# Mixing step of batches 1 to 3 with cosine and sine sums kept apart over half the columns

## The chip, the cores and the metric

The kernel runs on one NeuronCore of one Trainium2 chip. The metric is the device time of one execution in microseconds (us), measured beside the kernel before on the same chip. Before the change the median of three runs is 973.34 us (965.94 to 981.02).

## What is computed

The reference chains a recurrent attention layer, a Fourier mixing layer with a two-layer network, and a network that mixes tokens and then channels. The change touches the Fourier layer alone:

```python
X = np.fft.fft(x, axis=1)          # x: (4, 768, 320): batch, token, feature
X = np.fft.fft(X, axis=2)
mixed = np.real(X)
u = x + mixed
mu = mean(u, -1); var = mean((u - mu) ** 2, -1)
un = (u - mu) / np.sqrt(var + 1e-06)
out = u + np.maximum(un @ w_ch1, 0.0) @ w_ch2
```

The real part of the second transform is a cosine sum minus a sine sum. Over 320 output features the cosine sum is even (column j and column 320-j agree) and the sine sum is odd.

## The kernel before

The program is one list of some 4,500 operations. Each is declared with a cost and the data it reads and writes; the order in which all are issued, over all engines, is a table of base-36 numbers written out in the file (`ORDER`). An entry such as `+5,acc,0` is a filler: five products of an identity matrix (function `warm`, L54) into a PSUM bank that nobody reads. Each engine takes its instructions in that order, and waits on semaphores.

In time the program runs through these stages: the attention (to about 395 us); the first Fourier step and mixing of batch 0 (to 430.6); the channel network of the Fourier layer (430.6 to 682.5), in six groups of four 128-token tiles, each a chain of `hps` products (L1049, 8 of 512 columns), a relu on ScalarE (L1051), its low part on VectorE (L1052), and `acc` products (L1039, 12 of 320 columns); the token network (`tps`, `t2ps`, to 730); and the last channel network (`sa`, `sb`, `acc` L1075). Batches 1, 2 and 3 pass their Fourier step between the products of groups 0, 2 and 3. Each number is split into a high and a low part (fp32r), so that one exact product is three rounded ones.

Function `fft2` is the mixing step. Its loop makes four blocks `mix` for each batch. A block is eight matmuls of 322 columns into one PSUM bank of the pair `mm` (shared with `hps` and with the transposes `trp`): A0, A1 are the high and low parts of the cosine rows, A2, A3 those of the sine rows, A4 the 64 remaining rows, and T2 the table of cosines and sines in six slabs. VectorE then adds the block to the tile X, read straight from PSUM, and for all but part of the tiles a second time with the columns reversed (L952, seven adds for each batch; each also leaves the row sum). ScalarE squares and sums each tile (`sq`, L955). From the sums VectorE forms `v`, `y`, `q` and `nb` (L962 to L969), the shift and scale of the batch; `norm` and `trp` (L1020) use them to make the operand `cc` of the next group. Only batch 1 is followed at once by a group that needs it (group 1, at 481.5 us); batches 2 and 3 are needed one group later.

While this runs, the weights of the second network are decoded on VectorE and GpSimd (tiles `mdraw`, `mdt`, `mda`, `mdh`, L854 to L860). GpSimd also issues the loads of weights from DRAM (`wload`): T2 at 390 us, W1 (`W1t`) and W2 from 402 us.

Of the kernel before, what the change touches and what calls it, by code (L numbers as in the profile page):

```python
# [539 lines left out]
+10,y,0 7w:0 88:1 89 8b:1 8c 7z:1 8d dt 7x +1,y,0 85:0 ds bs bt 80 82:1 83 3b 86 8e 8f 7y 8g 8j 8i 8k hk 8h dy du dr dz 3c 3e 8w 84 81 3d 8x 8y +7,y,0  # L540
8z:1 90 95:0 96 98:1 99 9b:0 9c 92:1 93 9e:0 9f 9j 3f 3i 3j 9i 3g 3m 3h 3n 8a bw bv 87 3k dv dw c6 9a 3l 3o e0 hl hr dx e3 e1 e2 hm 9h hq hn ho mp hs
ms 3r 3p 9k 9o 9p 9q 9r 9s 9t 9u 9v 9w 9x 9y 42 43 9z a0 mt 91 +12,y,0 e4:1 e5 9n +2,y,0 e7:0 e8 c9 3q a1 a4 a2 a3 a5 a6 a8 a9 9l aa a7 +2,y,0 ed:1 bu
b5 b3 b8:2 b9 ba bb bc bd fi b6 e9 ab ad b7 ee ef ac 44 9m b4 ew +2,y,0 ej:0 ek el +3,y,0 be:0 +1,y,0 bf bg bh ea:1 eg:0 et ey:1 ez ae af bi bj +2,y,0
cb:2 +2,y,0 ce:0 ex ah qj eb 94 f0 +1,y,0 f1 e6 ag ai aj al hj hp eh en em ep 9d cc cd cf cg +2,y,0 ct:1 cm:2 cn co ch:0 ck cl ci cj cp cq f3 cr:0 f2
f4:1 f5 f6 +1,y,0 f7 cu ak am ap aq an at ao au eo es eq er hv cs cy:1 d6:0 cz cv:1 cw d0 d1 fy:0 hu ec fh eu ar as f8 d7 d8 ax ht ev g0 fv:2 of hw:0
i5:1 av 45 4a cx:0 ay aw b2 d9 fz 97 46 48 fx d2 i6 i7 i2:1 9g hx d3:0 f9 mq i3 i4 ib:1 az b0 b1 g4:0 d4 i8:0 gh:1 fw g1:1 ic id hz:1 47 49 4c 4d 4e
4g 4h 4b g6 i9 g5 ia hy gi g3 k0 gj i0 i1 if ie g2 d5 gc:2 gf gg df:0 ig dg dh di 4f 4i 4j gk dc:1 dd fj fk fl fm gl:0 gm g7:0 ga gb da nw ih k5:1
+2,m,0 k6 k7 k8 k9 ka ns +1,m,0 gn:1 go db +2,m,1 de:0 dj dk dl dn kh:0 ki g8 g9 k3 +1,m,0 fn:1 fo gd ge il im in io ip iq ir is it iu iv +2,y,0 kj:0
kk ei fp:1 fq h0:1 h1 h2 h3 dm l5:1 l2:0 k2 gx:0 gy l4 fr:0 gp:1 gq iw fs ft:1 fu mu dp l3 gs:0 l7 do gt gu gv k1 k4 l6 ix iy kp mv mw to kl:0 mr km
kb:2 kc kd ke gr:0 gw gz h4 kf kg lb:0 n0 iz ij n1 j1 h5 h6:1 n2 lc ko h9:0 nx:1 ld h7 kq j0 ha +1,t,0 h8:0 kr hb j2 hc l8:2 kt ii ik j5 hd l9 o9:1 oh  # L550
j3 la ny oa j6 nz o0 vq nu ob:0 j7 o1 mx o2 ls:1 ja oc n6:1 j4 od:0 he lt j8 oe hf n3:0 j9 ql jb ks qk ku:1 nv le:0 my kv je hg lo:0 hh mz lu:1 lj:2
4m lv qm n7 og kw:1 n4 lz:1 lq jc 4l n5 nt jd m0 +1,y,0 nc:0 lf kx m2 lm lw:1 4k nd m1 lg ky:1 lx nf:0 ln kz jf ng ji +1,y,0 l0:1 ni:1 lp lh n9:0 nh
o3:1 lr lk li o4 nj o5 na o6 nk qn l1 o7 nm ou:0 qo nl o8 m4:1 zi ow m7:0 m5 qp m8 +1,t,0 ly:0 qq jg md:1 qw ma jh no m3 m9 me qu ll m6 jj qv mg:0 4n
oi oj mb qs ox:2 qr mh jk nn mc mi qx:1 mj jl n8 ok oz np jo +1,y,0 r0:0 jp nr mf:0 js ov qy ol mk 4o nq jm pg:1 r1 jn ti:0 xg oy tq jq p0:1 pi tj jr
+1,m,0 r3:1 4p ju ph r6:0 qz ml r4 mm nb jt pj mo p3:0 r5 jv r7 mn p1 jz qt p2 4q vr r8 jw +5,y,0 om:0 vt +2,y,0 r9:1 tk:1 4s on rc:0 jy ra vu p6:2 jx
# [118 lines left out]
TC=416  # L674
# [6 lines left out]
def tables():  # L681
# [625 lines left out]
```

## Time and profile before

| | us |
|---|---|
| median of 3 runs | 973.34 |
| lowest, highest | 965.94, 981.02 |
| the profiled execution's own time | 981.04 |
| its span, first to last instruction | 979.3 |
| busy: TensorE (PE) | 926.0 (95%) |
| busy: VectorE (DVE) | 710.4 (73%) |
| busy: ScalarE (ACT) | 491.7 (50%) |
| busy: GpSimd (POOL) | 371.4 (38%) |

All durations below come from the profiled execution. An instruction's duration includes its passage through the engine's pipeline; how long a matmul holds up the next one is read from the difference between two starts. "x8" in a row of the timeline merges eight like instructions that follow each other.

### The profile page before, as it was taken

The numbers are of one execution on the slowest core, as the hardware profiler recorded it, in microseconds if no ns is written. First come the engines' busy times: TensorE is split into PE (matmuls) and PEld (weight loads), VectorE is DVE, ScalarE is ACT, GpSimd is POOL, SyncE is SP. The second block draws the span as 40 slices with busy tenths as digits, with TensorE's granted clock in tenths as the row PEclk, the third lists the DMA queues.
The fourth block names the chain that finished last, engine by engine and source line by source line (L and its number), as shares of the span: only waits on it lengthen the run. The fifth ranks groups of instructions, "written<-read, shape, count | busy, mean of one in ns | idle before, by whom it ended". The sixth has DMA issues, their size and how long they took to land.

```text
span 979.3 us, 24229 instructions
## 1 busy us (share of the span) xinstructions
PE 926.0 (95%) x9661; PEld 858.9 (88%) x9661; DVE 710.4 (73%) x1543; ACT 491.7 (50%) x1068; POOL 371.4 (38%) x498
## 2 busy tenths in 40 slices
PE   7568999999999999889999999999999999999998
PEld 6467888888898888779898998989999999999998
DVE  6798469798886936998978776562686876666554
ACT  5254688879788766352444443322324443433422
POOL 5121344535266355426265644254243213122110
PEclk9775699999999999999999999999999999999999
DMA  9877488989978799657344434349533212303000
GB/s 217 165 143 162 105 176 195 194 181 195 205 193 169 202 213 308 208 202 228 115 152 120 158 112 124 108 131 379 181 137 119 86 51 78 97 4 98 1 28 28
DMA packets 153840, 146.15 MB, mean 149 GB/s; under 512 B 101695, under 2 KB 127359, under 8 KB 152959
## 3 DMA queue, kind: packets, MB, share of 16 engines
q1 hardware_dynamic: 143743, 117.64, 47.1%
q0 software_dynamic: 9984, 26.96, 9.0%
q8 instruction: 76, 1.25, 0.6%
q14 instruction: 37, 0.30, 0.1%
HBM read 96.22 MB, written 43.58 MB: 143 GB/s over the span
## 4 chain that ended last, share of the span: by engine, by line
PE 71%; DVE 12%; DMA 7%; ACT 3%; issue 2%; SPq 1%; POOL 1%; DVEq 0%; ACTq 0%; POOLq 0%
PE acc L1075 12%; PE hps L1049 11%; PE acc L1039 10%; PE sb L1086 7%; PE sa L1086 5%; PE kg L216 4%; PE sc L406 3%; PE warm L54 3%; PE tps L1181 2%; PE t2ps L1194 2%; PE mix L949 2%; DVE pr L249 2%; DMA RT<-a 2%; DMA Mst<-Md 1%; SPq L134 1%
## 5 line engine op out<-in xcount | busy, mean ns | idle before, releaser
L1049 PE MATMUL hps<-cc,W1t 128*128 128x512 f32 x480 | 121.0, 395 | 0.1
L1039 PE MATMUL acc<-W,cc 128*128 128x320 f32 x720 | 116.0, 310 | 0.0
L1039 PEld LDWEIGHTS acc<-W,cc 128*128 128x128 f32 x720 | 109.2, 188 | 4.7 <-ACT mdh L838 0.3
L1049 PEld LDWEIGHTS hps<-cc,W1t 128*128 128x128 f32 x480 | 87.8, 188 | 16.9 <-PE hps L1049 0.5
L1099 POOL TENSOR_TENSOR C<-C,C 128x256 f32<-128x256 f32 x36 | 27.4, 761 | 173.0 <-DVE W1t L1092 115.3
L1051 ACT ACTIVATE cc<-hps 128x512 fp32r<-128x512 f32 x60 | 35.8, 597 | 107.0 <-PE hps L1049 107.0
L54 PE MATMUL warm<-ident 128*128 128x128 f32 x490 | 82.1, 307 | 2.6 <-POOL ident masks.py:199 2.0
L1052 DVE SCALAR_TENSOR_TENSOR cc<-hps,cc 128x512 fp32r<-128x512 f32 x60 | 41.3, 689 | 55.6 <-ACT cc L1051 55.5
L54 PEld LDWEIGHTS warm<-ident 128*128 128x128 f32 x490 | 71.2, 213 | 5.5 <-POOL ident masks.py:199 2.0
L225 POOL TENSOR_SCALAR_AFFINE_SELECT RT<-RT 64x384 f32<-64x384 f32 (+1 forms) x66 | 44.1, 687 | 80.8 <-ACT RT L136 79.7
L216 PE MATMUL kg<-am,bt 120*128 120x192 f32 x242 | 59.7, 388 | 15.1 <-ACT am L136 13.6
L416 POOL TENSOR_SCALAR_AFFINE_SELECT sc<-sc 64x384 f32<-64x384 f32 (+1 forms) x72 | 41.7, 579 | 79.1 <-ACT sc L136 75.6
L1093 DVE TENSOR_TENSOR C<-sb,C 128x256 f32<-128x256 f32 x108 | 44.2, 420 | 33.2 <-PE sb L1086 26.4
L1075 PE MATMUL acc<-v,W1t 128*128 128x320 f32 x432 | 67.4, 309 | 0.1
L1075 PE MATMUL acc<-vb,W1t 128*128 128x320 f32 x432 | 66.9, 309 | 0.0
L1091 ACT ACTIVATE W1t<-C 128x256 fp32r<-128x256 f32 x108 | 41.9, 413 | 45.4 <-DVE C L1093 36.4
L1075 PEld LDWEIGHTS acc<-v,W1t 128*128 128x128 f32 x432 | 63.7, 188 | 0.4 <-DVE W1t L1092 0.4
L1075 PEld LDWEIGHTS acc<-vb,W1t 128*128 128x128 f32 x432 | 63.7, 188 | 0.0
L216 PEld LDWEIGHTS kg<-am,bt 120*128 120x128 f32 x242 | 46.6, 224 | 18.8 <-ACT am L136 14.6
L1092 DVE SCALAR_TENSOR_TENSOR W1t<-C,W1t 128x256 fp32r<-128x256 f32 x108 | 46.6, 449 | 19.4 <-ACT W1t L1091 19.0
L406 PE MATMUL sc<-rm,VZd 120*128 120x192 f32 x264 | 57.8, 350 | 1.0 <-ACT sc L136 0.9
L859 POOL TENSOR_TENSOR mda<-mda,mdh 128x320 f32<-128x320 f32 (+2 forms) x32 | 31.2, 979 | 64.4 <-ACT mdh L856 48.3
(224 smaller groups left out, 2261.1 us busy)
## 6 DMA issues: line engine op xcount, KB each, us to landing
bt<-in_bkR_dram SPq DMA_DIRECT2D x12, 660.0 KB
mdraw<-in_moe_w_ch_dram SPq DMA_DIRECT2D x22, 320.0 KB
mdraw<-in_moe_w_ch_dram SPq DMA_DIRECT2D x16, 384.0 KB
dr_T<-Y SPq DMA_DIRECT2D x24, 256.0 KB
Z<-dr_T SPq DMA_DIRECT2D x6, 1024.0 KB
wS<-in_wR_dram SPq DMA_DIRECT2D x12, 335.2 KB
a<-in_aR_dram SPq DMA_DIRECT2D x12, 335.2 KB
RT<-a SPq DMA_DIRECT2D x36, 111.7 KB
```

The source lines that it names most:

```text
L54: for x in range(m): nc.tensor.matmul(t[:,128*(x%4):128*(x%4)+128],lhsT=ident,rhs=ident,start=True,stop=True)
L216: nc.tensor.matmul(ps[:,192*x:192*x+192],lhsT=bt[:,g+x].rearrange("p v t -> p (v t)"),rhs=am[:,:,g+x],start=True,stop=True)
L225: nc.gpsimd.affine_select(out=kv,in_=kv,pattern=[[0,3*m],[1,L]],compare_op=ALU.is_gt,fill=0.0,base=0,channel_multiplier=-1)
L406: for x,g in enumerate(gs): nc.tensor.matmul(ps[:,192*x:192*x+192],lhsT=VZd[:,g].rearrange("p v t -> p (v t)"),rhs=s.rm[:,:,g],start=True, ...
L416: nc.gpsimd.affine_select(out=o,in_=o,pattern=[[0,3*m],[-1 if rv else 1,L]],compare_op=ALU.is_gt,fill=0.0,base=L-1 if rv else 0,channel_mu ...
L1039: nc.tensor.matmul(s.pst(acc[x]),lhsT=a[:,sl],rhs=w2(w,m),start=(m==0 and n==0),stop=(m==MT-1 and n==2))
L1049: for n,(l,r) in enumerate(ops): nc.tensor.matmul(ps,lhsT=l,rhs=r,start=n==0,stop=n==7)
L1075: nc.tensor.matmul(s.pst(acc[x]),lhsT=a[:,sl],rhs=wv(w),start=(u==0 and y==0 and k==0),stop=(u==5 and y==1 and k==2))
L1086: for n,(y,x) in enumerate(((0,0),(0,1),(1,0),(2,2))): nc.tensor.matmul(R[r](),lhsT=va(q,y),rhs=S[:,x],start=first and n==0,stop=last and ...
L1091: s.act(256,lambda: nc.scalar.activation(out=Hh(y,c),in_=src(),func=AF.Relu),rd,[('Hh',z,y,c)],free=free)
L1092: s.dve(.33,lambda: V.scalar_tensor_tensor(out=Hl(y,c),in0=src(),scalar=0.0,in1=Hh(y,c).bitcast(F32),op0=ALU.max,op1=ALU.subtract),rd+[('H ...
L1093: def add(n,r,m,free): s.dve(.33,lambda: V.tensor_tensor(out=C(n),in0=R[r](),in1=C(m),op=ALU.add),[K[r],('C',m)],[('C',n)],free=free)
```

## The change

For batches 1 to 3 a block is formed differently. Its two products with A4 come first and are 324 columns wide: the table's slabs 4 and 5 are reloaded after batch 0 with a form in which the cosine rows fill columns 0 to 161 and the sine rows columns 162 to 323. Then three products with A0 and A1 go to columns 0 to 161 and three with A2 and A3 to columns 162 to 323, 162 columns each. ScalarE copies the sine half to SBUF (tile `ms`); VectorE forms `mx`, 161 columns as sum and 160 reversed columns as difference, each from the PSUM half and `ms`. The seven adds to X read `mx` in SBUF instead of PSUM. There is one `ms` and one `mx`, in free columns of the tile Y. The PSUM bank is free after the difference and the sum. Batch 0 keeps the old form. The reload is one more DMA, issued by GpSimd, which waits for batch 0's last block.

```diff
-            h=s.psum('mm',[128,384],"mix"); kp=('pm',h[0])
+            h=s.psum('mm',[128,384],"mix"); kp=('pm',h[0]); two=b>0
             def f(h=h,r=r,cs=cs):
-                A=t["A"]; T2=t["T2"]
+                A=t["A"]; T2=t["T2"]; ps=s.pst(h)
+                if two:
+                    for n in range(2): nc.tensor.matmul(ps[r,:324],lhsT=A[4][:,cs],rhs=T2[:,4+n],start=n==0,stop=False,skip_group_check=True)
+                    for o in range(2):
+                        for n,(aa,tb) in enumerate(((0,0),(0,1),(1,0))): nc.tensor.matmul(ps[r,162*o:162*o+162],lhsT=A[2*o+aa][:,cs],rhs=T2[:,2*o+tb,:162],start=False,stop=n==2,skip_group_check=True)
+                    return
...
+            if two:
+                z=0; mx=lambda: t["Y"][:,1536:1857]
+                ms=lambda: t["Y"][:,1857:2019]
+                s.act(162,lambda h=h,ms=ms: nc.scalar.activation(out=ms(),in_=s.pst(h)[:,162:324],func=AF.Copy),[kp],[('ms',z)],free=[h[0]])
+                s.dve(.22,lambda h=h,mx=mx,ms=ms: V.tensor_tensor(out=mx()[:,:161],in0=s.pst(h)[:,:161],in1=ms()[:,:161],op=ALU.add),[kp,('ms',z)],[('mx',z,0)],free=[h[0]])
+                s.dve(.22,lambda h=h,mx=mx,ms=ms: V.tensor_tensor(out=mx()[:,161:321],in0=s.pst(h)[:,159::-1],in1=ms()[:,159::-1],op=ALU.subtract),[kp,('ms',z)],[('mx',z,1)],free=[h[0]])
             def add(q,rows,cols):
-                s.dve(.46,lambda h=h: V.scalar_tensor_tensor(out=x(q,rows),in0=s.pst(h)[rows,cols],scalar=1.0,in1=x(q,rows),op0=ALU.mult,op1=ALU.add,accum_out=t["sm"][rows,q]),[kp]+xk(q)+['pend'],[('x',q,b),('sm',q)],free=[h[0]])
+                if two: s.dve(.46,lambda mx=mx: V.scalar_tensor_tensor(out=x(q,rows),in0=mx()[rows,cols],scalar=1.0,in1=x(q,rows),op0=ALU.mult,op1=ALU.add,accum_out=t["sm"][rows,q]),mk+xk(q)+['pend'],[('x',q,b),('sm',q)],port=True)
...
         s.first[b]=False
+        if b==0: s.wload(lambda: t["T2"][:,4:6],s.T2d[:,6:],[],['T2s'],1.0)
```

The table `ORDER` is new throughout, so operations of every stage stand in other places than before, in the attention too (there the first difference on PE comes after some 65 rows, on VectorE after 15). Fillers number 245 before and 248 now. Three places matter for the prediction. Line numbers after the change are larger: `hps` is L1065, `acc` L1055, the old form of `mix` L956, the new one L950 and L952.

TensorE ahead of the channel network's first group; `trp` is the last transpose for group 0, and `mix` here is the first block of batch 1. Before:

```order
L1020 MATMUL trp<-ident,Y 128x128 x4
L54 MATMUL warm<-ident 128x128 x4
L949 MATMUL mix<-T_5456,A_5457 128x322 x2
L949 MATMUL mix<-T_5456,A_5458 128x322
L949 MATMUL mix<-T_5456,A_5459 128x322 x2
L949 MATMUL mix<-T_5456,A_5460 128x322
L949 MATMUL mix<-T_5456,A_5461 128x322 x2
L1049 MATMUL hps<-cc,W1t 128x512 x16
```

Now:

```order
L1036 MATMUL trp<-ident,Y 128x128 x8
L54 MATMUL warm<-ident 128x128 x6
L1065 MATMUL hps<-cc,W1t 128x512 x16
L950 MATMUL mix<-T_5453,A_5458 128x324 x2
L952 MATMUL mix<-T_5453,A_5454 128x162 x2
L952 MATMUL mix<-T_5453,A_5455 128x162
L952 MATMUL mix<-T_5453,A_5456 128x162 x2
L952 MATMUL mix<-T_5453,A_5457 128x162
```

The block has moved behind the first two `hps`. Further on in group 0, five fillers behind the fifth `hps` and three ahead of batch 1's second block are gone; between the blocks of batch 2 there are two fillers now, and one between those of batch 3, where there were none; at the start of group 1 there are seven instead of four.

VectorE at the end of batch 1's mixing; `X,sm<-..., 32x320` is its last add to X. Before:

```order
L1052 SCALAR_TENSOR_TENSOR cc<-hps,cc 128x512
L952 SCALAR_TENSOR_TENSOR X,sm<-mix,X 32x320
L855 SCALAR_TENSOR_TENSOR mda_4890<-mdraw_4888,mdt_4889 128x384
L858 SCALAR_TENSOR_TENSOR mdt_4885<-mdraw_4884,mdt_4885 128x384
L962 TENSOR_SCALAR v<-ss 128x6
```

Now:

```order
L857 SCALAR_TENSOR_TENSOR mda_4891<-mdraw_4889,mdt_4890 128x384
L962 TENSOR_TENSOR Y<-mix,Y 128x161
L963 TENSOR_TENSOR Y<-mix,Y 128x160
L929 TENSOR_TENSOR A_5455<-psA_6261,A_5454 128x208
L966 SCALAR_TENSOR_TENSOR X,sm<-Y,X 32x320
L929 TENSOR_TENSOR A_5457<-psA_6256,A_5456 128x208
L1068 SCALAR_TENSOR_TENSOR cc<-hps,cc 128x512
L978 TENSOR_SCALAR v<-ss 128x6
```

Sum and difference stand ahead of the add, with one step of the next batch between; the add's first operand is Y (that is `mx`).

GpSimd, where it issues the loads of W1 and W2. Before:

```order
L796 DMA W1t<-m10h 128x1280
L859 TENSOR_TENSOR mda_4894<-mda_4894,mdh_4895 128x320
L860 TENSOR_TENSOR mda_4894<-mda_4894,mdt_4893 128x320
L796 DMA W1t<-m10l 128x1280
L859 TENSOR_TENSOR mda_4890<-mda_4890,mdh_4891 128x320
L796 DMA W_5577<-m11h 128x1600
```

Now:

```order
L798 DMA W1t<-m10h 128x1280
L862 TENSOR_TENSOR mda_4895<-mda_4895,mdt_4894 128x320
L798 DMA T_5453<-in_T_dram 128x648
L798 DMA W1t<-m10l 128x1280
L798 DMA W_5622<-m11h 128x1600
```

The reload of T2's two slabs stands ahead of the last load of W1.

## Rows read from the trace of the kernel before

**Rows 1.** The page, part 1: busy us, share, instructions by engine

```profile
PE 926.0 (95%) x9661; PEld 858.9 (88%) x9661; DVE 710.4 (73%) x1543; ACT 491.7 (50%) x1068; POOL 371.4 (38%) x498
```

**Rows 2.** Busy time by stage: stretch, length, then engines as the first line names

```profile
core 0: us, PE busy (x) PEld busy (x) DVE busy (x) ACT busy (x) POOL busy (x), PEclk, DMA share, GB/s
0.00:395.00 395.00, 354.36 (x5831) 317.26 (x5831) 299.41 (x573) 272.88 (x510) 163.03 (x255) 0.91 0.83 190
...
430.60:461.00 30.40, 30.31 (x166) 26.61 (x166) 27.41 (x56) 10.03 (x23) 16.26 (x17) 1.00 0.61 186
461.00:481.50 20.50, 19.02 (x133) 17.31 (x131) 18.11 (x46) 9.05 (x23) 8.50 (x8) 1.00 0.54 184
481.50:571.20 89.70, 89.70 (x526) 81.15 (x526) 71.87 (x156) 39.54 (x92) 46.95 (x46) 1.00 0.44 138
571.20:682.50 111.30, 111.30 (x625) 100.30 (x625) 60.94 (x121) 35.33 (x73) 47.87 (x56) 1.00 0.55 160
```

**Rows 3.** What PE waited for from 430 us on: us in total, times, longest

```profile
PE trp L1020 <- DVE cc L1024: 1.3, 1, 1.3
```

**Rows 4.** Timeline of PE at batch 1: start, us, line, operation, idle before

```profile
468.04 1.36 PE L949 MATMUL mix<-T,A 128*128 128x322 f32 x8
469.23 0.35 PE L901 MATMUL psA<-T,Xh 128*128 128x416 f32 x1
469.43 0.26 PE L901 MATMUL psA<-T,Xl 128*128 128x208 f32 x1
469.52 0.37 PE L901 MATMUL psA<-T,Xh 128*128 128x416 f32 x1
...
479.68 0.66 PE L1020 MATMUL trp<-ident,Y 128*128 128x128 f32 x4 [1.34 <-DVE cc L1024]
...
481.48 3.97 PE L1049 MATMUL hps<-cc,W1t 128*128 128x512 f32 x16
```

**Rows 5.** Timeline in group 0, at the two places with fillers

```profile
443.30 0.69 DVE L1052 SCALAR_TENSOR_TENSOR cc<-hps,cc 128x512 fp32r<-128x512 f32 x1
...
445.77 1.28 PE L54 MATMUL warm<-ident 128*128 128x128 f32 x10
...
446.80 2.00 PE L1039 MATMUL acc<-W,cc 128*128 128x320 f32 x12
...
461.37 0.83 PE L54 MATMUL warm<-ident 128*128 128x128 f32 x6
...
461.95 1.44 PE L949 MATMUL mix<-T,A 128*128 128x322 f32 x8
```

**Rows 6.** Single lines: count, ns least/median/most, first and last start, forms

```profile
L952 DVE SCALAR_TENSOR_TENSOR X<-mix,X x28: 475/488/498, 411.1 to 571.5; 128x320 f32<-128x320 f32 x20, 96x320 f32<-96x320 f32 x4, 32x320 f32<-32x320 f32 x4
...
L927 DVE TENSOR_TENSOR A<-psA,A x24: 354/369/379, 400.0 to 554.4; 128x208 fp32r<-128x208 f32 x16, 64x208 fp32r<-64x208 f32 x8
...
L926 ACT ACTIVATE A<-psA x24: 327/354/367, 398.8 to 552.8; 128x208 fp32r<-128x208 f32 x16, 64x208 fp32r<-64x208 f32 x8
...
L858 DVE SCALAR_TENSOR_TENSOR mdt<-mdraw,mdt x32: 418/492/1169, 368.4 to 652.8; 128x320 f32<-128x320 uint16 x22, 128x256 f32<-128x256 uint16 x6, 128x384 f32<-128x384 uint16 x4
...
L855 DVE SCALAR_TENSOR_TENSOR mda<-mdraw,mdt x32: 414/492/1737, 366.7 to 651.5; 128x320 int32<-128x320 int32 x22, 128x256 int32<-128x256 int32 x6, 128x384 int32<-128x384 int32 x4
```

**Rows 7.** Batch 0's last blocks, first hps, last load of W1 (issue; us to landing)

```profile
412.18 2.63 PE L949 MATMUL mix<-T,A 128*128 128x322 f32 x16 [1.37 <-DVE X L952]
...
430.57 4.21 PE L1049 MATMUL hps<-cc,W1t 128*128 128x512 f32 x16
...
415.59 0.57 POOL L796 DMA_DIRECT2D W1t<-m10l  x1
...
W1t<-m10l POOLq DMA_DIRECT2D x3, 640.0 KB, 5.4
```

**Rows 8.** Busy time in two stretches of the attention (columns as in Rows 2)

```profile
100.00:110.00 10.00, 10.00 (x173) 8.75 (x169) 4.90 (x10) 4.35 (x8) 2.84 (x4) 0.50 0.37 87
...
120.00:130.00 10.00, 10.00 (x223) 8.56 (x223) 3.82 (x9) 9.71 (x18) 4.08 (x8) 1.00 0.80 186
```

More of the change, by code (lines that the diff above doesn't have):

```diff
@@ L540 @@
[L540 to L543, printed above, removed]
@@ L665 @@
+3kv 3l8 3le 3lc 3lh 3li 3kw 3kx 3lr 3l1 3l2 3ld 3lp 3lq 3lj 3l0 3ls 3lm 3ln 3lo 3lk 3ll 3lf 3lg 3lu 3lv 3lt 3lw 3lz 3m0 3m1 3m2 3lx 3ly 3m3 3m4
 """
@@ L705, in tables @@
     T2[:64,4]=h; T2[64:,4]=h; T2[:64,5]=l
+    for k,v in ((6,h),(7,l)): T2[:33,k,:162]=v[:33,:162]; T2[33:64,k,162:]=v[33:,:162]
+    T2[64:,6]=T2[:64,6]
     return T1.astype(np.float32),T2
@@ L763, in begin @@
         s.P.stage=('mlp',0)
-        s.wload(lambda: s.t["T2"],s.T2d,['mid'],['T2'],3.0)
+        s.wload(lambda: s.t["T2"],s.T2d[:,:6],['mid'],['T2','T2s'],3.0)
         go=s.go; go(s.fft,0)
@@ L947, in f @@
                 ops=[(A[0],0,128),(A[0],1,128),(A[1],0,128),(A[2],2,128),(A[2],3,128),(A[3],2,128),(A[4],4,128),(A[4],5,128)]
                 for n,(aa,tb,K) in enumerate(ops):
-                    nc.tensor.matmul(s.pst(h)[r,:322],lhsT=aa[:,cs],rhs=T2[:,tb],start=n==0,stop=n==7)
-            s.pe(1.18,f,[('A',a) for a in range(5)]+['T2','pend'],[kp],alloc=h[0],cols=2570)
+                    nc.tensor.matmul(ps[r,:322],lhsT=aa[:,cs],rhs=T2[:,tb,:322],start=n==0,stop=n==7)
+            s.pe(.84 if two else 1.18,f,[('A',a) for a in range(5)]+['T2','T2s','pend'],[kp],alloc=h[0],cols=1616 if two else 2570)
@@ L951, in add @@
             def add(q,rows,cols):
-                s.dve(.46,lambda h=h: V.scalar_tensor_tensor(out=x(q,rows),in0=s.pst(h)[rows,cols],scalar=1.0,in1=x(q,rows),op0=ALU.mult,op1=ALU.add,accum_out=t["sm"][rows,q]),[kp]+xk(q)+['pend'],[('x',q,b),('sm',q)],free=[h[0]])
+                if two: s.dve(.46,lambda mx=mx: V.scalar_tensor_tensor(out=x(q,rows),in0=mx()[rows,cols],scalar=1.0,in1=x(q,rows),op0=ALU.mult,op1=ALU.add,accum_out=t["sm"][rows,q]),mk+xk(q)+['pend'],[('x',q,b),('sm',q)],port=True)
+                else: s.dve(.46,lambda h=h: V.scalar_tensor_tensor(out=x(q,rows),in0=s.pst(h)[rows,cols],scalar=1.0,in1=x(q,rows),op0=ALU.mult,op1=ALU.add,accum_out=t["sm"][rows,q]),[kp]+xk(q)+['pend'],[('x',q,b),('sm',q)],free=[h[0]])
@@ L1129, in f @@
             s.mk(p,[128,6,256],"k1",F32R,2); s.mk(p,[128,2,768],"k2",F32R,2)
-        ks=[('T1',k) for k in (0,1,'f')]+['T2','dd','Ds']+[(v,k) for v in ("FP","FM","Xh","Xl") for k in range(3)]+[('ef',k,z) for k in range(3) for z in range(2)]+[('sd',z) for z in range(2)]
+        ks=[('T1',k) for k in (0,1,'f')]+['T2','T2s','dd','Ds']+[(v,k) for v in ("FP","FM","Xh","Xl") for k in range(3)]+[('ef',k,z) for k in range(3) for z in range(2)]+[('sd',z) for z in range(2)]
         ks+=[('A',a) for a in range(5)]+[('mraw',j,x) for j in range(3) for x in range(2)]+[(v,j) for v in ('mdt','mda','mdh') for j in range(3)]
```

262 lines of the change are left out of this document (133 added, 129 removed).

## The prediction

> **What bounds the kernel now.** I read four views, in this order. The page's first part says that TensorE is busy for 95% of the span and VectorE for 73% [rows 1]; that is an average over stages, so the next view is busy time by stage [rows 2]. In the channel network, where the change lies, PE is busy for 30.31 of 30.40 us, then for 19.02 of 20.50, and then without a gap to 682.5. In the attention it is busy for 354.36 of 395 us at a mean granted clock of 0.91; there other engines and DMAs lead. The list of waits says what the missing 1.5 us are: of the waits from 430 us on, the longest by far is one of 1.3 us, of the transposes `trp` for VectorE [rows 3], at the start of group 1 [rows 4]. So what is taken from PE's work after 430 us shortens the program by as much, except at that one place: group 1 needs batch 1's statistics, and what ends last there is the chain from batch 1's mixing over ScalarE and VectorE to `trp`. There VectorE has little room: 27.41 of 30.40 and 18.11 of 20.50 us [rows 2], some 5.4 us free in 50.9. Batches 2 and 3 are mixed in groups 2 and 3 and first needed a group later, and VectorE has 17.8 us free between 481.5 and 571.2 [rows 2].
>
> **A block on PE.** From the start of a block's first matmul to that of the next work are 469.23-468.04 = 1.19 us for eight of 322 columns [rows 4], 0.149 us each, 0.46 ns a column. The new block has two of 324 columns, 0.30 us, and six of 162. The trace has no 162-column matmul of this kind. If time goes by columns, one takes 0.075 us and the block 0.75. The nearest row, a 208-column matmul with as large a load of weights, lets its successor start after 469.52-469.43 = 0.09 us; at 0.095, if the time does not fall further with fewer columns, the block takes 0.87. I take the middle, 0.81, since 208 is near to 162 and 208 columns at 0.46 ns give 0.096, so nothing but columns shows at that size. The gain is 0.38 a block, **4.6 us** in twelve (3.8 to 5.3).
>
> Beside this stands a rule of the Trainium skill, TensorE: Matmul & The Clock Gate, section LDWEIGHTS: a load of weights takes its number of columns divided by 1.2, in ns, whatever the number of rows. By it 128 columns take 107 ns, the block (an estimate from that page) 0.94 us and the gain 3.0. The 0.09 us above [rows 4] speak against it here, as a load belongs to each of those matmuls.
>
> **Fillers and the bank.** Eight fillers ahead of batch 1's mixing go. Their rows are 446.80-445.77 = 1.03 us for five (ten matmuls in the trace) and 461.95-461.37 = 0.58 for three [rows 5]. They cover no wait: the work behind the first five, an `acc`, needs VectorE's low part of an `hps`, which began at 443.30 and took 0.69, 1.8 us ahead of the fillers [rows 5]. That is **1.6 us** of PE's time. Three new fillers stand between blocks of batches 2 and 3, at 0.21 each **0.6 us** lost. They mark a real wait: the fourth block needs the bank of the second, free only when ScalarE's copy (0.35 by a 208-column row) and two steps of VectorE (up to 0.37 each by a row that also reads PSUM and SBUF) are through [rows 6], 1.1 us against 0.81 for the block between. The fillers cover most of that; I add **0.3 us** over both batches.
>
> **The end of batch 1.** Here the new form is longer by one ScalarE copy and two VectorE steps, 0.35+2x0.37 = 1.1 us, and by a hand-over; **1.3 us** later than PE alone would have it, and nothing hides it. VectorE's eight additional steps for batch 1 are 2.4 to 3.0 us (0.30 to 0.37 each). PE arrives 4x0.38+1.6 = 3.1 us earlier, so of VectorE's 5.4 free us 2.3 are left: it is 0.1 to 0.7 short by itself. To this comes a change of kind. The adds that read PSUM take 475 to 498 ns, all 28 of them; steps of like size that read both operands from SBUF, with GpSimd at work on the same decode, have the same median (492) but go up to 1169 and 1737 [rows 6]. Seven adds for each batch change from the first kind to the second. None stretched adds nothing; all seven by 1169-492 = 0.68 add 4.7 us. I take two stretched, and in all **1.5 us** (0.1 to 5.4): the median says that most are not. In batches 2 and 3 the 17.8 us free absorb such stretches.
>
> That the kinds differ so is what SBUF — State Buffer of the Trainium skill, section Who interferes with whom, leads one to expect: a VectorE instruction with two SBUF inputs shares its second read port with GpSimd, one with at most one does not. The trace agrees, 498 against 1737 ns at most [rows 6].
>
> **Moved at no cost.** Batch 1's first block goes behind two `hps`; it is on PE's path in both places. The reload of T2 (a third of a MB) makes GpSimd wait for batch 0's last block, which starts about 1.3 us into the pair at 412.18 and ends near 414.8; the last load of W1, now behind it, went at 415.59 and such a load lands 5.4 us later, while the first `hps` starts at 430.57 [rows 7]. That is 9 us of cover for the load; past it each us of delay would cost a us. The reload itself, at most half such a load, is needed only two `hps` later. ScalarE's twelve copies, 0.35 us each, lie in its idle time: it works 19 of the 50.9 us around batch 1 [rows 2]. The attention's rows are the same work in another order; I put that at nothing, since I can't read a direction from rows.
>
> **Sum.** -4.6 -1.6 +0.6 +0.3 +1.3 +1.5 = -2.5 us. The profiled execution took 981.04 us (span 979.3, with 1.7 around it) and would take 978.5; it is 7.7 us above the median of the runs shown, so against the median the forecast is 973.3-2.5 = **971 us**. By the bounds of the two open prices it is 968.7 (block at 0.75, VectorE 0.1) to 975.5 (0.87, 5.4).
>
> **The rivals.**
> *All of it stays* (968): VectorE's steps fit into its gaps, and only the longer chain costs: -4.6-1.6+0.9+1.3 = -4.0, and with the block at 0.75 -4.8. For it: the median of 492 [rows 6]. Against it: only 5.4 us free.
> *VectorE becomes the bound at batch 1* (976, slower than before): adds and sums stand behind GpSimd. With all seven adds stretched to 1169 VectorE is 5.4 us late instead of 1.5, 974.7; to 1737, 978.7. I price it at 976. It decides once the lateness passes 1.5+2.5 = 4.0 us, seven adds stretched by 0.5 on average. For it: stages that are 90% full [rows 2] and the tails in rows 6; against it: the decode steps can be the ones to wait.
> *The narrow product is not as cheap as its columns* (972): the fillers' 128-column matmuls hold PE 1.03/10 = 0.103 each, with as large a load of weights [rows 5]; at that price a block takes 0.92, the gain is 3.2, and the sum -1.1. Against it: the 0.09 of a 208-column one.
> *The order of the attention decides* (961 or 981): from 100 to 110 us PE is busy all the time at a granted clock of 0.50, its lower level of 1.2 GHz; from 120 it has 1.00 [rows 8]. A stretch of 10 us at full work and half clock holds 5 us that a risen clock returns. New rows there can bring the rise two such stretches earlier or hold it off as long, 10 us either way. For it: everything behind the first 65 rows of PE is reordered, and the three runs of one and the same program already lie 15 us apart. Against it: the work and the number of fillers are nearly the same.
>
> **How the numbers follow.** Forecast 0.42; all stays 0.14; VectorE 0.17; the narrow product 0.12; the attention 0.15, half each way. The range, 960 to 982, takes in the first four with the bounds 968.7 to 975.5 and the scatter of the runs (about 7 us to either side of the median), and the nearer part of the fifth; what is outside is about half of that case and a tail of the others, less than 2 in 10. The likeliest case alone is 967 to 975. Two per cent, about what a measurement of this kernel can tell from no change, is 19.5 us: below 953.9 or above 992.8. None of the cases reaches that far; the attention with the scatter on top could, 0.03 on each side.
>
> **What would show it.** In the profile after: PE still without gaps from 430 to 682 except at group 1; blocks at 0.75 to 0.87 us from start to start; the stage from the first `hps` to the first `tps` 2 to 3 us shorter than its 251.9 (the three stretches and the last of rows 2, 430.6 to 682.5); at group 1 a wait for VectorE longer than 1.34 us; adds to X from `mx` with a median near 490 ns and some far above. It would be wrong if the blocks take 0.9 or more, if that wait exceeds 4 us, if PE waits at batch 1's first block for the reload, or if the first `hps` starts more than some 5 us from 430.57, which would be the attention's doing.

## The result, and the profile after

The changed kernel takes 980.79 us (median of 20 runs, 973.67 to 991.34), the kernel before beside it 974.44 (20 runs, 963.98 to 982.54). The ratio is 1.0073, 95% interval 1.0044 to 1.0101: slower by 4 to 10 us, too little to count at 2%. The forecast was 2.5 us faster, so the sign is wrong. The profiled execution after took 979.91 us (span 978.2); that of before, 981.04, lay 6.6 above its median, so the two spans must not be compared as they stand.

The page of the changed kernel, part 1, answers to [rows 1]: VectorE has 12 us more to do, TensorE 4 us less.

```profile
PE 921.8 (94%) x9667; PEld 853.6 (87%) x9667; DVE 722.5 (74%) x1567; ACT 495.3 (51%) x1080; POOL 370.1 (38%) x499
```

Busy time of the changed kernel from the first `hps` to the first `tps`, columns as in [rows 2]:

```profile
425.20:680.80 255.60, 249.47 (x1449) 223.51 (x1448) 190.97 (x398) 98.43 (x223) 120.67 (x128) 1.00 0.52 156
```

The stage is 255.6 us long where the four stretches of [rows 2] have 251.9. VectorE works 191.0 instead of 178.3. TensorE, which had lost 1.6 us in the whole stage, now loses 6.1. The list of what TensorE waited for from 425 us on in the changed kernel (engine, line, releaser: us in total, times, longest), which answers to [rows 3], says to whom:

```profile
PE mix L950 <- DVE Y L963: 1.8, 1, 1.8
PE mix L950 <- DVE cc L1068: 1.1, 1, 1.1
PE trp L1036 <- DVE cc L1040: 1.1, 1, 1.1
PE psA L918 <- DVE A L930: 0.7, 1, 0.7
PE mix L950 <- DVE cc L1040: 0.7, 1, 0.7
PE t2ps L1210 <- DVE X L1212: 0.6, 1, 0.6
PE trp L1036 <- DVE cc L1068: 0.3, 1, 0.3
PE hps L1065 <- DVE cc L1068: 0.3, 1, 0.3
PE hps L1065 <- DVE Y L963: 0.2, 1, 0.2
```

Nine waits stand there, all for VectorE, where before had one of 1.3. Only the first and the last are for the new sum and difference (L963). Two more are at mixing blocks, for a bank of `mm` that VectorE still reads; five are at rows that the edit does not touch (`t2ps` belongs to the token network, behind the stage).

The timeline of TensorE in the changed kernel, one new block in group 0 (answers to [rows 4]):

```profile
456.70 0.46 PE L950 MATMUL mix<-T,A 128*128 128x324 f32 x2
456.99 0.80 PE L952 MATMUL mix<-T,A 128*128 128x162 f32 x6
457.62 1.96 PE L1055 MATMUL acc<-W,cc 128*128 128x320 f32 x12
```

457.62-456.70 = 0.92 us instead of 1.19: 0.29 for the wide pair and 0.63 for the six narrow ones, 0.105 each, where the forecast's block of 0.81 us left 0.085 for each. In the other blocks (but for the last, behind which TensorE waits) the six take 0.63 to 0.64 us too and the pair 0.29 to 0.41, so a block takes 0.92 to 1.04 us.

The timelines of VectorE (DVE), GpSimd (POOL) and TensorE (PE) in batch 2 of the changed kernel, around the longest wait (start, us, engine, line, operation, idle before). Batch 2 is mixed at the end of group 1 and batch 3 at the end of group 2, in both kernels, one group earlier than the description ahead of the prediction has it:

```profile
515.36 1.17 DVE L966 SCALAR_TENSOR_TENSOR X<-Y,X 128x320 f32<-128x320 f32 x1
...
516.46 1.29 DVE L966 SCALAR_TENSOR_TENSOR X<-Y,X 128x320 f32<-128x320 f32 x1
...
517.68 1.14 DVE L829 TENSOR_SCALAR mdt<-mdraw 128x384 int32<-128x384 int32 x1
518.74 0.48 DVE L1126 TENSOR_TENSOR X<-acc,X 128x320 f32<-128x320 f32 x1
519.14 0.31 DVE L962 TENSOR_TENSOR Y<-mix,Y 128x161 f32<-128x161 f32 x1
519.38 0.31 DVE L963 TENSOR_TENSOR Y<-mix,Y 128x160 f32<-128x160 f32 x1
...
515.18 1.00 POOL L823 TENSOR_TENSOR mdt<-mda,mda 128x384 f32<-128x384 f32 x1
516.26 1.14 POOL L823 TENSOR_TENSOR mdraw<-mdt,mda 128x384 f32<-128x384 f32 x1
517.36 1.24 POOL L823 TENSOR_TENSOR mdt<-mda,mda 128x384 f32<-128x384 f32 x1
...
515.64 0.54 PE L950 MATMUL mix<-T,A 128*128 128x324 f32 x2
516.03 0.80 PE L952 MATMUL mix<-T,A 128*128 128x162 f32 x6
516.66 0.49 PE L950 MATMUL mix<-T,A 128*128 128x324 f32 x2
516.99 0.80 PE L952 MATMUL mix<-T,A 128*128 128x162 f32 x6
517.62 0.42 PE L54 MATMUL warm<-ident 128*128 128x128 f32 x2
519.83 0.54 PE L950 MATMUL mix<-T,A 128*128 128x324 f32 x2 [1.79 <-DVE Y L963]
```

Two adds of the first block, which read `mx` and X from SBUF, take 1.17 and 1.29 us while GpSimd works on SBUF without a break; a decode step (L829) takes 1.14 instead of the 0.35 that it has elsewhere. The three are 2.3 us longer than usual. So the sum of the second block (515.64 to 516.66) starts only at 519.14, 2.5 us after the block's end. Its difference ends at 519.69, and only then is its bank free for the fourth block. Over all adds of the changed kernel (line, count: least/median/most ns):

```profile
L966 DVE SCALAR_TENSOR_TENSOR X<-Y,X x21: 480/489/1295, 433.7 to 571.9; 128x320 f32<-128x320 f32 x15, 96x320 f32<-96x320 f32 x3, 32x320 f32<-32x320 f32 x3
```

The median is 489 where [rows 6] had 488, and the longest 1295 where it had none above 498. Six of the 21 take 0.82 to 1.29 us, two in each batch, all six beside work of GpSimd; the 14 with no work of GpSimd beside them take 0.48 or 0.49.

**Where to measure from.** In all profiles the granted clock is at its upper level through nearly all of the stage (0.99 or 1.00 on average), so its length repeats better than the time ahead of it. The first `hps` is a poor start, because the change puts a block behind it. Batch 0's last pair of blocks has the old form in every kernel. From its start to the first `tps` before takes 682.39-412.18 = 270.2 us [rows 7], the changed kernel 680.81-408.81 = 272.0:

```profile
408.81 1.43 PE L956 MATMUL mix<-T,A 128*128 128x322 f32 x8
...
680.81 2.36 PE L1197 MATMUL tps<-W1t,k 128*128 128x320 f32 x15
```

This length is called the stretch below. Three profiles of before's order and block behind the attention (before, e4, e13) give 270.2, 268.4 and 270.7, mean 269.8; three of the changed one (after, e5, e18) 272.0, 271.3, 271.7, mean 271.7. So 1.9 us of the loss lie here, and some 0.4 behind (297.2 against 296.9 us to the end of the span, means of the same profiles). The rest lies ahead. All of this holds to about 1 us: e4, whose attention has the new order, is 2 us shorter than the other two, most of it ahead of group 0. From the first work of group 0 on (batch 1's first block before, the first `hps` now) the six take 253.1, 253.0, 253.7 and 255.6, 255.8, 255.3 us, a loss of 2.3.

### The profile page after: what moved, and what is told of

It reads as the page before. It is cut to its first block, busy times and chain, and to the rows that moved or that the text cites. A ratio compares the mean times of both kernels' runs of the same rounds, so it can differ in the third digit from the quotient of the medians.

```text
span 978.2 us, 24270 instructions
## 1 busy us (share of the span) xinstructions
PE 921.8 (94%) x9667; PEld 853.6 (87%) x9667; DVE 722.5 (74%) x1567; ACT 495.3 (51%) x1080; POOL 370.1 (38%) x499
## 5 line engine op out<-in xcount | busy, mean ns | idle before, releaser
L1065 PE MATMUL hps<-cc,W1t 128*128 128x512 f32 x480 | 121.1, 396 | 0.4 <-DVE cc L1068 0.3
L1055 PE MATMUL acc<-W,cc 128*128 128x320 f32 x720 | 116.0, 310 | 0.1
L1055 PEld LDWEIGHTS acc<-W,cc 128*128 128x128 f32 x720 | 109.1, 188 | 4.4 <-DVE cc L1068 0.4
L1065 PEld LDWEIGHTS hps<-cc,W1t 128*128 128x128 f32 x480 | 87.7, 188 | 17.5 <-issue 0.6
L1068 DVE SCALAR_TENSOR_TENSOR cc<-hps,cc 128x512 fp32r<-128x512 f32 x60 | 41.3, 688 | 50.9 <-ACT cc L1067 50.8
L225 POOL TENSOR_SCALAR_AFFINE_SELECT RT<-RT 64x384 f32<-64x384 f32 (+1 forms) x66 | 41.0, 641 | 88.0 <-ACT RT L136 86.8
```

What stands on the lines that cost most here:

```text
L1055: nc.tensor.matmul(s.pst(acc[x]),lhsT=a[:,sl],rhs=w2(w,m),start=(m==0 and n==0),stop=(m==MT-1 and n==2))
L1065: for n,(l,r) in enumerate(ops): nc.tensor.matmul(ps,lhsT=l,rhs=r,start=n==0,stop=n==7)
L1068: s.dve(.61,lambda: nc.vector.scalar_tensor_tensor(out=t["hl"][z],in0=s.pst(h),scalar=0.0,in1=t["hh"][z].bitcast(F32),op0=ALU.max,op1=ALU. ...
```

## The experiments

Theory A: the edit itself costs. The bank is held longer, and VectorE has more to do where it has little room. Theory B: the new order costs, and the edit saves what its products save. The first four runs cross the two.

**e1, e16: the old block in the new order.** The products, copy, sum and difference are before's; what stays is the table ORDER.

```diff
- ORDER of before
+ ORDER of the changed kernel without ms, mx and the reload of T2
```

> The eight 322-column products and the adds straight from PSUM of the kernel before, in the order of the changed kernel (fillers and all; the copy, the sum and the difference and the second load of T2 are taken out; in two blocks the adds stand where the sum stood, since the bank is wanted by then). Medians so far: before 974.4, changed 980.8. Theory A (the edit costs: the bank of a block is held through a copy and two steps, and VectorE has 9 us more to do in a stage in which it is nearly full): back at 974 to 976. Theory B (the new order costs, whatever the block is, and the block itself saves its 3.2 us on TensorE): about 980.8 + 3.2 = 984. In between, both.

Measured: 974.74 us, ratio 1.0037 (1.0007 to 1.0067); stretch 271.0. The order alone costs. The waits of TensorE from 418 us on in this kernel are those of the changed one without the two on L963:

```profile
PE mix L948 <- DVE cc L1051: 1.1, 1, 1.1
PE trp L1019 <- DVE cc L1023: 1.1, 1, 1.1
PE psA L915 <- DVE A L927: 0.7, 1, 0.7
PE t2ps L1193 <- DVE X L1195: 0.6, 1, 0.6
PE mix L948 <- DVE cc L1023: 0.5, 1, 0.5
PE trp L1019 <- DVE cc L1051: 0.3, 1, 0.3
PE hps L1048 <- DVE cc L1051: 0.3, 1, 0.3
```

The 1.1 us at a block is batch 1's first, now behind two `hps`: both hold a bank of `mm`, and the block gets one only when VectorE has read the first. It is not the reload that it waits for, since this kernel has none. Neither theory's number alone fits.

> The first experiment again, beside the two below. From batch 0's last block of mixing to the end of the sixth group it takes 271.0 us, the changed kernel 271.3 to 272.0, so nearly as long; but its median was 974.7 and the changed kernel's 980.8, twice, so that all but one of these 6 us lie ahead of that block, where the two kernels have the same rows in the same order on every engine. If that is a thing of the kernel: again 974 to 976. If it was the draw of the runs: 977 to 981.

Measured, on another chip: 977.55, ratio 1.0026 (0.9989 to 1.0064), stretch 270.8. The ratio repeats within its interval; the time itself was 2.8 us longer. From the first work of group 0 on, e1 and e16 take 255.4 and 255.2 us, 2 us more than before.

**e2: the new block in the old order.**

```diff
- ORDER of the changed kernel
+ ORDER of before; ms behind each block, mx ahead of its first add
+ the loop declares the blocks of batches 1 and 2 in another sequence
```

> The new block with its copy, sum and difference, in the order of the kernel before, its fillers kept; copy right behind the block, sum and difference right ahead of the block's first add, and held back only where the single buffer of the sum asks for it. Theory A: 978 to 982, since bank and VectorE are loaded as in the changed kernel. Theory B: the block's gain is seen alone, 974.4 - 3.2 = 971, at most 973 with what the copy adds.

Measured: 980.37, ratio 1.0074 (1.0034 to 1.0114), stretch 275.6. In an order not made for it the edit costs 5.8 us in the stretch, mostly as waits for VectorE's low parts (`acc` 1.5 us in three waits, `psA` 1.9 in two) and for the difference (1.0 at a block, 0.7 at `hps`). With e1: the new order costs 1.6 us in the stretch (mean of e1, e16 and e17 271.4) and saves the new block 3.9. The two do not add.

**e3, e4: the attention's order exchanged.**

```diff
- entries of ORDER ahead of the channel network (own)
+ the same entries of the other kernel
```

> The changed kernel, but all that stands ahead of the mixing of batch 0 (the attention, weight decoding and first Fourier products) in the order of the kernel before. If the new order of the attention costs (a front about 2 us longer in the changed kernel by its medians and one profile): 978 to 979. If the whole loss lies from the first mixing on: 980.8, within 1.

Measured: 983.43 (6 runs), ratio 1.0126 (1.0074 to 1.0178), stretch 275.6. By its profile the changed rest behind before's attention is worse than behind its own: the stretch is 3.6 us longer than the changed kernel's, 2.0 of it ahead of the first `hps`, and the span behind the stretch 2.1 us longer. The intervals of the two ratios overlap.

> The mirror image: the kernel before, but with the attention in the changed kernel's order. If the new order of the attention costs: 976 to 977. If not: 974.4, within 1.

Measured: 974.22, ratio 1.0025 (0.9991 to 1.0060), stretch 268.4. The attention's new order alone: no more than some 6 us, perhaps nothing.

**e5: the changed kernel again.**

> The changed kernel again, on the chip of the runs beside it. The two profiles give 253.0 us from the first block of batch 1 to the end of the sixth group before and 255.6 after, and 0.5 more behind it: 3.1 us. The medians are 6 to 8 apart, and the mean granted clock of the changed kernel's 20 runs was 0.970 against 0.976 of before. If that clock is the chip's or the hour's, here it is as high as before's and the time is 976 to 977; if it belongs to the kernel, 980 to 981 again with a clock near 0.970.

Measured: 980.87, ratio 1.0069 (1.0036 to 1.0102), mean granted clock of its runs 0.971 against 0.975 of before; stretch 271.3. The loss repeats, the lower clock too.

**e6, e10, e11: products and sums taken apart.** e6 is before with the narrow products alone, e10 the same in the new order (that is, e1 with them), e11 the changed kernel with the wide products.

```diff
-T2[:,tb]  into [r,:322]      (eight times)
+T2[:,2*o+tb,:162]  into [r,160*o:160*o+162]      (six of the eight)
```

> The kernel before, its order untouched; only the six products of 162 columns in place of 322 (the sine part is laid 160 columns on), and the adds still read PSUM straight away. The sum and the difference are left out, so what is added to X is not the mixing. What the products alone give: twelve blocks shorter by 0.27 to 0.28 us each if a 162-column product takes 0.105 us there too, so stage 251.8 - 3.0 = 248.8 and time 972.9 - 3.2 = 969.7; by columns alone (0.075) 968.3. If TensorE then waits for VectorE instead, up to 972.9.

Measured: 973.37, ratio 0.9978 (0.9943 to 1.0014); stretch 267.7, 2.1 shorter than the 269.8.

> The first experiment (the old adds in the order of the changed kernel; stage 255.4) with the narrow products and nothing else; sum and difference are left out, so the output is not the mixing. Only the products' gain is left in: 12 x 0.27 = 3.2 off, stage 252.1, if TensorE is bound there; 253.5 to 254 if half is given back at the next wait for VectorE, as in the sixth experiment (1.6 of 3.0 came through).

Measured: 971.19 (8 runs), ratio 0.9987 (0.9936 to 1.0038); stretch 268.7.

> The changed kernel with its six products 322 columns wide again; copy, sum, difference, adds and order stay (what they add up is then not the mixing). If the copy, sum and difference cost the same whatever the products take: stage 255.6 + 3.2 = 258.8. If TensorE waits there for VectorE in either case, the longer products lie in the waits: 256 to 257, and the wait of 1.8 us at batch 2 shrinks.

Measured: 986.76 (2 runs), ratio 1.0112 (1.0049 to 1.0175); stretch 273.4; the wait for the difference in batch 2 shrinks to 1.15 us. In the new order the four stretches are:

| | adds from PSUM | copy, sum, difference |
|---|---|---|
| wide products | 271.4 | 273.4 |
| narrow products | 268.7 | 271.7 |

The upper left entry is the mean of e1, e16 and e17 (271.0, 270.8, 272.5), the lower right that of after, e5 and e18; the others are one profile each. The narrow products bring 2.7 and 1.7 us, the sums cost 2.0 and 3.0: nothing is left. Twelve times 0.27 us would be 3.2. Of the rest, e6 has 0.6 us in new waits; e10 waits as long as e1, and where its rest goes the rows do not show. The sums' cost lies in group 1, where batch 2 is mixed: 1.9 us with narrow products (after against e10) and 1.4 with wide ones (e11 against e1), while group 0 has 0.1 and 0.0 and group 2 0.5 and 0.2.

**e12: how narrow a product pays.**

```diff
-162 columns
+(96,128,256)[b-1] columns for batch b
```

> The changed kernel with products of 96 columns in batch 1, 128 in batch 2 and 256 in batch 3 in place of 162 (so the output is not the mixing). From start to start of six: if a product is never shorter than some 0.105 us beside its 128x128 weights, 0.63 us at 96 and at 128 columns as at 162, and 6 x 0.118 = 0.71 at 256. If time goes by columns: 0.27, 0.35 and 0.71.

One run (981.7 us). TensorE's timeline, one block of batch 1, one of 2 and one of 3, each with the row that follows:

```profile
465.10 0.77 PE L953 MATMUL mix<-T,A 128*128 128x96 f32 x6
465.70 0.42 PE L903 MATMUL psA<-T,Xh 128*128 128x416 f32 x1
...
518.26 0.78 PE L953 MATMUL mix<-T,A 128*128 128x128 f32 x6
518.88 0.51 PE L950 MATMUL mix<-T,A 128*128 128x324 f32 x2
...
564.93 0.88 PE L953 MATMUL mix<-T,A 128*128 128x256 f32 x6
565.65 0.60 PE L1037 MATMUL trp<-ident,Y 128*128 128x128 f32 x4
```

Six take 0.60, 0.62 and 0.72 us: 0.100, 0.103 and 0.120 each, with 0.105 at 162 columns. Below some 220 columns, 0.105 us at the 0.47 ns a column of the 256, the width hardly counts.

**e7, e14: fillers of before taken out**, all behind batch 1's first block in e7, the two in group 0 in e14.

```diff
-+5,ps,0 ... +3,ps,0        (e14: eight fillers; e7 takes out eight more entries, ten fillers)
```

> The kernel before without its 15 fillers that come after the first block of batch 1 (eight in front of group 1, five in group 1, and the later ones); nothing else is moved. If TensorE is bound there by its own work, as the prediction has it: eight of 0.13 us and more gone, 1.0 to 1.6 us faster, 971.5. If the fillers stand in time in which TensorE would wait anyway (the trp wait of 1.34 us grows by what they took): same, 972.9. If the granted clock falls without them: slower.

Measured: 970.24, ratio 0.9942 (0.9905 to 0.9980); stretch 270.0. Group 0 is 1.1 us shorter, group 1 1.5 longer. The total is better than its profile accounts for: its stretch is 0.2 us shorter than before's, and ahead of it nothing was changed (see below). It lacks 18 of the 245 fillers, not the 15 of the expectation. Stretches of e7 at the start of group 1 (us, then TensorE busy, granted clock, DMA share, GB/s):

```profile
474.90:480.20 5.30, 5.30 (x18) 0.68 0.03 9
480.20:488.00 7.80, 7.80 (x45) 1.00 0.17 50
```

Behind waits of 1.56 and 0.40 us that no filler covers, the mean granted clock of these 5.3 us is 0.68: for 3.4 of them, from 475.2, it is at the lower of its two levels (1.2 GHz, 0.50).

> The kernel before without the two fillers in the first group (five and three matmuls of the warm kind) that stand among batch 1's Fourier products; the fillers around the trp that waits ahead of group 1 stay, so do those behind the stage. If the seventh experiment was read rightly (1.1 us gained in the first group, 1.5 lost in the second to a granted clock of 0.76 behind the longer wait): stage 250.7, TensorE's clock full in the second group, 1 us faster or same. If the clock falls here too: 252 to 253.

Measured: 971.56, ratio 0.9980 (0.9940 to 1.0019); stretch 269.5, group 0 49.9 us instead of 50.9, clock 1.00 through group 1. Its profile shows a reason to be shorter than before, 1 us in group 0, which the timing can't confirm. The fillers took 1.6 us; 0.54 of it is back as a wait of an `hps` for a bank, two blocks behind the place of the second filler entry. In group 3 another 0.75 us is lost, with a wait of 0.6 us of an `hps` for VectorE's low part, so that from the first work of group 0 to the first `tps` only 0.2 us is left (252.9 against 253.1).

**e8, e9: the sum elsewhere.** In e8 (old order) ScalarE copies both halves and GpSimd sums; in e9 (new order) ScalarE copies both and VectorE sums from SBUF.

```diff
-ACT: ms = sine half;  DVE: mx = PSUM +/- ms
+ACT: ms = sine half, mz = cosine half;  POOL (e8) or DVE (e9): mx = mz +/- ms
```

> The new block in the order of the kernel before (as the second experiment), but ScalarE copies both halves (two copies of 162), which frees the bank, and GpSimd forms the sum and the difference from the copies. VectorE is back at before's steps, except that its adds read SBUF. If VectorE's additional 0.64 us a block and the bank it holds were the cost of the second experiment (5 us over before): 970 to 973. If it is the adds that read SBUF beside a working GpSimd, or the chain grown longer at the end of a batch: 977 to 981.

Measured: 988.70 (6 runs), ratio 1.0131 (1.0083 to 1.0180), stretch 284.5. Worse than any: GpSimd takes 0.54 and 0.62 us for a sum and a difference, VectorE's adds wait 10 us for it, and what stands behind them on VectorE waits too (one `psA` for 3.9 us).

> The changed kernel, its order kept; ScalarE copies both halves (two copies of 162, the second into a tile of its own), and VectorE forms sum and difference from the two copies in SBUF, so the bank is free after the copies, whatever VectorE still has to do. In the changed kernel TensorE waits 1.8 us in batch 2's fourth block for the difference and 0.16 at batch 3's end. If the bank held until the difference is the cost, these go and the first hps to first tps takes 253.6 to 254.2 instead of 255.6 to 255.8. If VectorE's own lateness is the cost, the wait turns up at the next trp or hps and the stage stays at 255.5 or grows, since sum and difference now read SBUF beside GpSimd.

Measured: 983.36, ratio 1.0082 (1.0042 to 1.0121), stretch 272.6. The wait of 1.8 us is gone and group 1 is 1.3 us shorter, but group 2 is 2.2 longer: waits of TensorE from 425 us on in e9, among them

```profile
PE psA L918 <- DVE A L930: 1.6, 2, 0.9
PE acc L1056 <- DVE cc L1069: 1.5, 2, 0.8
```

So freeing the bank earlier does not shorten the stage. But sum and difference read only SBUF here, and they stretch too (median 328 and 325 ns, most 1177), so this run does not part the held bank from VectorE's lateness.

**e15: VectorE's time alone.** e1 with two steps of 161 columns behind each block's adds, read by nobody.

```diff
+for n in range(2): dve(mx = X[:161] + X[159:320])
```

> The first experiment (old block, adds from PSUM, the changed kernel's order; stage 255.4) with two VectorE steps of 161 columns behind each block's adds, from X to a scratch that nobody reads: VectorE's time of the sum and the difference, without their place in the chain and without a bank held. If VectorE's time alone is the cost of the changed block (255.6 with narrow products, 253.1 with narrow products and no sum): 255.4 + 2.5 = 258. If it is the chain, copy to sum to difference to add, or the held bank: 255.4 to 256.

Measured: 985.83 (2 runs), ratio 1.0137 (1.0058 to 1.0215); stretch 277.1, 5.7 us over the 271.4. The idle steps (ns as above, 24 of them, 9.7 us in all):

```profile
L961 DVE TENSOR_TENSOR Y<-X x24: 320/329/1061, 429.1 to 571.2; 128x161 f32<-128x161 f32 x24
```

A block's own chain is not longer in this kernel, and each us of VectorE costs 0.6 us of the stretch, at `acc` in group 0 above all (2.6 us in three waits). That is more than the sums cost, and in another place: group 0 is 4.0 us longer than in e1, group 1 1.5. So VectorE's time alone can make the stage longer, but e15 does not show that it is what the sums cost in batch 2.

**e13, e17, e18: the larger table.** Before, e1 and the changed kernel with the other's table of cosines.

```diff
-T2: 6 pieces of 322        (e18 the other way round)
+T2: 8 pieces of 324 in DRAM, 324 wide in the tile
```

> The kernel before with nothing changed but the table of cosines: 324 columns wide in the tile and eight pieces in DRAM, as in the changed kernel (what lies behind it in SBUF moves by 48 bytes); the products stay 322 wide and nothing else is loaded or done. If the 2.5 to 3 us that the changed kernel loses ahead of its first hps (mean granted clock 0.970 against 0.975) come from where the data lie: clock near 0.970 and 976 to 977. If not: as before, 974 to 975, with stage 251.8.

Measured: 973.26, ratio 1.0007 (0.9970 to 1.0044), stretch 270.7.

> The same with the changed kernel's table (eight pieces of 324 in DRAM, 324 wide in the tile) and nothing else of it. If where the data lie makes the first 400 us longer together with the new order: 979 to 981 at a mean granted clock near 0.970. If not: as the run above.

Measured: 978.30, ratio 1.0042 (1.0006 to 1.0079), stretch 272.5.

> The changed kernel with the table and the tile of before (six pieces of 322; the sine part 160 columns on, the second load of T2 fetches two of the old pieces, so what it mixes is not the reference's), all else as changed. If the table makes the front long: 974 to 976. If not: 980 to 981 again.

Measured: 977.79, ratio 1.0021 (0.9981 to 1.0061), mean clock 0.972 beside 0.973 of before; stretch 271.7. e17 is as slow as e16 beside it, so the table makes nothing long; e18 has the changed kernel's stretch and, at the clock of before beside it, a third to a half of its loss, with an interval that takes in none at all and nearly all of it.

## Why the prediction was wrong

**A block on PE: mis-sized.** 0.92 us, not 0.81. The step "nothing but columns shows at that size" failed: it was read from one 208-column matmul behind a 416-column one, 0.09 us [rows 4]. In rows of equals 96, 128 and 162 columns take 0.100 to 0.105 (e12, after), more than that 208-column matmul. Why it is shorter behind a longer neighbour no run here shows. The Trainium skill's TensorE: Matmul & The Clock Gate, section LDWEIGHTS, gives the number of their columns divided by 1.2, in ns, for a load of weights: 107 here, an estimate from that page. The trace agrees within 7% (0.100 us at 96 columns), and the prediction set the rule aside on that one row. The rival of the narrow product, given 0.12, had the block at 0.92 from the fillers' rows and was right about the block, though not about the time. Of its 3.2 us, 1.7 to 2.7 arrive. Forecast -4.6, measured -2.2.

**Fillers and the order: failed.** The prediction took 1.6 us for eight fillers, gave 0.6 for three new ones and put all other moves at nothing, "since I can't read a direction from rows". Taking out eight at these two places gives 1.0 in group 0 and 0.2 over the stage (e14). And the order as a whole costs 1.6 us in the stretch with the old block in it (e1, e16, e17 against 269.8): forecast -1.0, measured +1.6. It moves blocks, transposes and `hps` to places where VectorE has not yet freed their bank, and the wait of `trp` for VectorE at group 1 is hardly shorter, 1.1 instead of 1.3. One of the new waits was in reach: a block behind two `hps`, with two banks in `mm`, has to wait for VectorE's reading of the first, 1.1 us here. The prediction put this move at no cost.

**Bank, chain and VectorE: near in size by luck, wrong in place.** Forecast 0.3+1.3+1.5 = 3.1; measured 2.0 to 3.0. At batch 1's end, where 2.8 of the 3.1 were to arise, two of the seven adds did stretch, as the prediction took, by 1.6 us together; but the wait at group 1 did not grow, and in group 0 the sums cost 0.0 to 0.1 us. They cost 1.4 to 1.9 in group 1, at batch 2, where the prediction had 0.3 for the bank over both batches and let 17.8 free us absorb stretched adds: free time over 90 us does not help when blocks follow each other within some 3 us. The kind of cause holds: adds from SBUF are stretched beside GpSimd with the median unmoved (489, most 1295). The Trainium skill, SBUF — State Buffer, section Who interferes with whom, says that a VectorE instruction with two SBUF inputs contends with a GpSimd instruction that reads SBUF; the trace agrees, all six adds above 0.5 us run beside GpSimd. Whether the held bank or VectorE's queue by itself makes the wait in batch 2 stays open: e9 does not part them. The rival "VectorE becomes the bound" named the stretched adds and VectorE's lateness, but for batch 1.

**The attention.** The first `hps` came 5.3 us earlier than in before's profile, at the edge of the bound that the prediction named. That says little: the last scan of the attention (VectorE, L179) starts at 278.57 in before's profile, at 272.49 in the changed kernel's, and anywhere from 264 to 281 in the 20 profiles of this study, in both orders. From this scan to batch 0's last pair eight profiles with before's attention give 132.3 to 134.7 us, mean 133.5, and twelve with the new one 133.1 to 139.7, mean 135.5. So the new order seems to cost another 2.0 us there; e4's total does not contradict it, nor prove it. The prediction put the attention's rows at nothing in its sum, and looked for a cost or a gain in the first rise of the clock alone.

At least part of the 2.0 us is a fall of the clock much later, in batch 0's first Fourier step. The rows of TensorE in the changed kernel, then its granted clock around them (stretch, length, busy, granted clock, DMA share, GB/s), and below the last dots the same wait in before:

```profile
395.37 0.36 PE L903 MATMUL psA<-T,Xl 128*128 128x208 f32 x1 [2.53 <-DVE Xl L888]
...
396.27 3.48 PE L54 MATMUL warm<-ident 128*128 128x128 f32 x16
399.51 0.44 PE L903 MATMUL psA<-T,Xh 128*128 128x416 f32 x1
...
392.00:396.00 4.00, 1.47 (x11) 1.00 0.61 183
396.00:399.40 3.40, 3.40 (x18) 0.50 0.72 267
399.40:405.50 6.10, 4.06 (x33) 1.00 0.45 136
...
399.24 0.37 PE L901 MATMUL psA<-T,Xl 128*128 128x208 f32 x1 [0.71 <-DVE Xl L886]
```

TensorE waits 2.53 us for VectorE where before has 0.71; then the clock is at its lower level (0.50), and sixteen fillers take 399.51-396.27 = 3.24 us, 0.20 each, where at the upper level they take some 0.11. The mean granted clock between scan and pair is 1.00 in all eight profiles with before's attention and 0.95 to 0.99 in all eleven with the new order throughout, and the longest of them, 137.0 to 139.7 us in e5, e16 and e17, have 0.95 to 0.98. e4 has the new attention alone and the same wait (2.4 us), but its clock stays at 1.00, so what decides about the fall is not settled.

**The sum.** Stretch: -2.2 (products) +2.5 (sums) +1.6 (order) = +1.9; attention +2.0; behind +0.4; together 4.3 us of the 6.3 between the medians, at the lower end of the interval of 4 to 10. Against the forecast of -2.5, the products miss 2.4, the order 2.6 in the stretch and 2.0 ahead of it. The timings of the old block in the new order agree: e1, e16 and e17 have ratios of 1.0037, 1.0026 and 1.0042, mean 3.4 us, where 1.6 and 2.0 make 3.6.

**What stays open.** Some 2 us, and what brings the clock down. The mean granted clock of the changed kernel's runs was 0.970 and, in e5, 0.971; before had 0.975 beside e5 and 0.976 beside e1. In e18 and before beside it the clock was the same, and the loss 3 us, between the medians. One kernel's total follows this clock on the whole: of the 29 runs of before beside e1 the one at 0.986 took 968.5 us, the two at 0.965 981.6 and 984.0. In the profiles it is, besides the fall shown above, the stretch from 80 to 120 us in which the clock reaches its upper level earlier or later: 0.58 and 0.65 for its two halves in before's, 0.78 and 1.00 after, 0.97 and 1.00 in e1, though e1 and the changed kernel have the same rows on every engine there. The later fall does not settle it either: e1 has it too, and the runs of e1 have a mean clock of 0.976. e7, with before's attention unchanged, came out some 5 us faster than its stretch explains. Whether the changed kernel draws the late rise more often, or did so by chance in 32 runs, these runs do not settle; there is no sign that the table (e13, e17) or the attention's order alone (e4) makes it.

## What to carry to other kernels

Price a narrower matmul from neighbours as narrow as itself: beside 128x128 weights a product of 96 columns costs nearly what one of 162 does. Work moved from TensorE to the engine that empties its banks has to be paid at the densest few microseconds of that engine, not over its average, and operands moved from PSUM to SBUF change their price if GpSimd is at work. And a new table of the order is a change of its own: cross it with the edit (old in new, new in old) before the edit gets the blame or the credit.

## What the runs showed of the hardware

- A run of 128x128-weight products in fp32r goes at 0.100, 0.103, 0.105 and 0.120 us each for 96, 128, 162 and 256 columns (e12; 162 in the changed kernel).
- Fillers that cover no time of their own can still pay: without those around a wait of 1.3 us, the granted clock behind it fell to 0.50 for 3.4 us, and group 1 took 1.5 us longer (e7); with them it stayed at 1.00 (before, e14).
- An add of 320 columns with both operands in SBUF takes 0.48 or 0.49 us with GpSimd idle and up to 1.29 beside it (changed kernel); with one in PSUM never above 0.50 (before).
